# Batch 2's 1/rms by full matmuls with ones in place of column tiles and spreading DMAs, with a new order of the pieces

## The chip, the cores and the metric

The kernel runs on one core of one Trainium2 chip. The metric is the device time in microseconds (us) of one execution; the time before is the median of three runs.

## The reference

Per batch and head, an attention without softmax: kv = kᵀv (64 x 64), out = q·kv, divided by its root mean square over the head's 64 columns and scaled by g. The heads side by side are x; a channel mix follows.

```python
kv  = einsum('bhsd,bhse->bhde', k, v)
out = einsum('bhsd,bhde->bhse', q, kv)
x   = out / sqrt(mean(out * out, -1) + 1e-06) * g_norm      # heads side by side: (8, 576, 512)
x_prev = x one row later, zeros in front
xk = mu_k * x + (1 - mu_k) * x_prev;  xr = mu_r * x + (1 - mu_r) * x_prev
kk = maximum(xk @ w_k, 0.0);  v = kk * kk @ w_v;  r = sigmoid(xr @ w_r)
return r * v
```

Sizes: 8 batches, 8 heads, 576 rows, head width 64; 512 columns, 1024 in the hidden layer. Inputs and output are float32.

## The kernel before

The attention goes by batch (b = 0 to 7), each in two halves z of four heads, and for some steps in two parts i of 288 rows. The mix goes by group of 512 rows (g = 0 to 8). Group g needs the batches that its rows lie in: group 2 needs batches 1 and 2, group 3 batches 2 and 3, group 4 batches 3 and 4.

The code declares named pieces with their dependencies (`add`), and `plan.emit` issues them in the order of the words in `ORDER`. There is no other scheduler: each engine and each DMA queue works through its own pieces in that order, so a piece that waits holds up those behind it on the same engine. A suffix @A or @D puts a piece on ScalarE or VectorE. The words:

- `ldh.k`, `ldh.v`: batch 0's first half as float32 (SyncE's queue), and `cst.*`, the casts of it. `ld.*`: the other loads (GpSimd's queue, each waits there until its buffer is free); `ld.q0.zb` is the second half of a half's q.
- `kv`: kᵀv on TensorE (L274). `kc`: copy out of PSUM. `ks`: matmuls with a permutation (L280). `kd`: copy of the result. `tq`: q transposed on VectorE (L367). `u`: q·kv, transposed (L291).
- `uc`: u times g from PSUM into uT (L134 on ScalarE, L136 on VectorE). `sq`: squares (L389, ScalarE).
- `ss`: sums of squares by head, on TensorE. `rs`: 1/rms by one ScalarE instruction of 128 x 576 (L297). `mul`: x = uT * rs (L415; batch 0 from PSUM, L411). `d`: difference of neighbouring rows (L309). `mk`, `mr`: d times mu - 1. `xk`, `xr`: the blended inputs (L322; batch 0 L329).
- `k{g}.{fc}`: xk @ w_k (L517; group 0 L492, in parts). `relu` (L475, ScalarE), `ksq` (square, VectorE). `r{g}.{ci}`: xr @ w_r (L544). `sig` (L554, ScalarE). `v{g}.{ci}.{part}`: times w_v (L564). `out`: product (L577, L591). `st`: store (L466, SyncE).
- `z:512` and `zz`: matmuls of zeros that add nothing, while the first loads come (L460). `table`: first load of ScalarE's function table.

PSUM gives four buffers ("ps") that all pieces on TensorE share.

The sums of squares are done in one of two ways, by `CB`:

- Batches below CB: a full 128 x 128 matrix `ones` (1/64 within each head) sums the squares and puts the sum on all 64 partitions of its head. Batch 1 has four pieces `ss1.0` to `ss1.3`, each two matmuls of 288 columns (L418), and four passes `rs1.0` to `rs1.3`. The result lies as `mul` needs it.
- Batches from CB on: eight matmuls with the 128 x 32 matrix `heads` write four column tiles side by side (L398), so one piece `ss2` holds all heads and one pass `rs2` does all into `rsc`. Then `sp2.0` and `sp2.1` spread it over the partitions: four DMAs each on SyncE's queue (L440), 72 KB each. `mul2.z` waits for `sp2.z`.

CB is 2 before.

Of the kernel before, what the change touches and what calls it, by code (L numbers as in the profile page):

```python
# [56 lines left out]
def kernel(  # L57
# [283 lines left out]
    def attention(b):  # L341
# [64 lines left out]
        for z in range(NZ):  # L406
# [27 lines left out]
            ps_ = []  # L434
            if b >= CB:
                def spread(_, z=z, rs=rs):
                    for y in range(2):
                        for e in range(2):
                            r = 32 * (2 * z + y)
                            nc.sync.dma_start(out=get(rs)[64 * e:64 * e + 64, y, :],  # L440
                                              in_=rsc.t[r + e:r + 32:2, :].unsqueeze(1).to_broadcast([16, 4, S]))
# [191 lines left out]
```

## Time and profile before

| | us |
|---|---|
| median of 3 runs | 199.29 (199.22 to 199.31) |
| the profiled execution | 199.39 |
| its span | 197.5 |
| TensorE busy | 188.0 (95%) |
| VectorE busy | 134.0 (68%) |
| ScalarE busy | 127.0 (64%) |

The span is what the trace covers; 1.89 us of the execution lie around it. Times in the trace count from the span's start. PE is TensorE, DVE VectorE, ACT ScalarE, POOL GpSimd, SP SyncE; SPq is SyncE's DMA queue. Where a matmul record is missing from the trace, the timeline shows a gap of 0.16 us.

### The profile page before, as it was taken

The page shows a single profiled execution, that of the slowest core. Times are in us where ns is not written, and L with a number is a line of the kernel's source. Part 1 is how long each engine was busy: PE and PEld are TensorE (multiplying, and loading weights), DVE is VectorE, ACT ScalarE, POOL GpSimd, SP SyncE. Part 2 cuts the span into 40 slices and gives each one's busy share as a digit, 9 for nine tenths or more (in the row PEclk, how much of TensorE's full clock was granted, in tenths as well). Part 3 has the DMA queues.
Part 4 walks back from the last instruction along what each step waited for, and adds up shares of the span by engine and source line. Part 5 has one row for each costly group of instructions (what it writes and reads, how often), then busy time and mean ns, then how long its engine had stood idle before and what let it go on. Part 6 is the DMA issues. An engine that isn't in the chain of part 4 may idle for free.

```text
span 197.5 us, 4233 instructions
## 1 busy us (share of the span) xinstructions
PE 188.0 (95%) x1736; PEld 93.2 (47%) x1760; DVE 134.0 (68%) x227; ACT 127.0 (64%) x166; POOL 24.6 (12%) x44
## 2 busy tenths in 40 slices
PE   7987999999998999999999999999999999999992
PEld 2445864443534544344556554444444444444451
DVE  3389979888749699964997949876398440431272
ACT  3365599569989579889895876795518463342300
POOL 7842433041303000000000000000000000000000
PEclk9999999999999999999999999999999999999999
DMA  6999999999999999999632404413506003002226
GB/s 219 214 206 216 198 198 208 212 204 214 212 238 263 225 233 280 229 214 262 251 110 60 113 5 113 131 37 81 150 0 240 25 0 110 0 0 106 94 90 244
DMA packets 21192, 30.63 MB, mean 155 GB/s; under 512 B 1964, under 2 KB 14516, under 8 KB 21172
## 3 DMA queue, kind: packets, MB, share of 16 engines
...
q8 instruction: 14, 0.23, 0.5%
...
q14 instruction: 6, 0.05, 0.1%
...
## 4 chain that ended last, share of the span: by engine, by line
PE 73%; DMA 14%; DVE 6%; ACT 2%; issue 2%; SPq 1%; POOL 0%; DVEq 0%; ACTq 0%
PE ps L517 25%; PE ps L564 25%; PE ps L544 12%; DMA q<-in_q_dram 11%; PE ps L460 4%; DMA rs<-rsc 3%; PE ps L492 2%; PE ps L291 2%; PE ps L274 2%; DVE xT L411 1%; DVE qT L367 1%; ACT relu L475 1%; DVE xk L329 1%; DVE d L309 1%; PE ps L398 1%
## 5 line engine op out<-in xcount | busy, mean ns | idle before, releaser
L564 PE MATMUL ps<-w_v,sqk 128*128 128x512 bf16 (+1 forms) x286 | 66.0, 373 | 1.0 <-issue 0.6
L517 PE MATMUL ps<-xk,w_k 128*128 128x512 bf16 (+1 forms) x280 | 59.1, 355 | 1.4 <-DVE xk L322 0.7
L475 ACT ACTIVATE relu<-ps 128x1024 bf16<-128x1024 f32 x36 | 36.7, 1025 | 24.4 <-PE ps L517 18.5
L564 PEld LDWEIGHTS <-sqk 128*128 128x128 bf16 x296 | 28.3, 98 | 32.6 <-issue 1.8
L532 DVE TENSOR_TENSOR sqk<-relu 128x1024 bf16<-128x1024 bf16 x32 | 21.6, 686 | 29.6 <-ACT relu L475 22.4
L517 PEld LDWEIGHTS <-w_k 128*128 128x128 bf16 x288 | 27.2, 98 | 27.9 <-issue 1.8
L544 PE MATMUL ps<-w_r,xr 128*128 128x512 bf16 x140 | 33.8, 379 | 0.2
L554 ACT ACTIVATE sig<-ps 128x1024 bf16<-128x1024 f32 x18 | 18.5, 1025 | 15.9 <-DVE out L577 7.8
L577 DVE TENSOR_TENSOR out<-ps,sig 128x1024 f32<-128x1024 f32 x16 | 19.5, 1219 | 11.2 <-issue 5.7
L389 ACT ACTIVATE sq<-ps 128x576 bf16<-128x576 f32 x32 | 20.2, 652 | 4.1 <-PE ps L291 2.2
L544 PEld LDWEIGHTS <-xr 128*128 128x128 bf16 x144 | 13.7, 98 | 16.0 <-issue 0.7
L367 DVE STREAM_TRANSPOSE qT<-q 128x576 f32<-128x576 f32 (+1 forms) x20 | 14.7, 761 | 3.7 <-DMA q<-in_q_dram 3.5
...
L134 ACT ACTIVATE md<-d,cols 128x576 bf16<-128x576 bf16 x20 | 14.2, 769 | 1.7 <-DVE d L309 1.5
L309 DVE TENSOR_TENSOR d<-xT 128x1152 bf16<-128x1152 bf16 (+1 forms) x18 | 12.4, 691 | 0.4
L134 ACT ACTIVATE uT<-ps,cols 128x576 bf16<-128x576 f32 x16 | 11.7, 744 | 1.2 <-PE ps L291 1.2
L415 DVE TENSOR_TENSOR xT<-uT,rs 128x1152 bf16<-128x1152 bf16 x14 | 10.4, 744 | 2.1 <-DMA rs<-rsc 1.1
L136 DVE TENSOR_SCALAR md<-d,cols 128x576 bf16<-128x576 bf16 x36 | 11.3, 363 | 0.2
L136 DVE TENSOR_SCALAR uT<-ps,cols 128x576 bf16<-128x576 f32 x12 | 9.6, 814 | 2.7 <-ACT sq L389 2.5
L322 DVE TENSOR_TENSOR xk<-md,xT 128x1152 bf16<-128x1152 bf16 x14 | 10.5, 756 | 1.2 <-ACT md L134 0.9
L322 DVE TENSOR_TENSOR xr<-md,xT 128x1152 bf16<-128x1152 bf16 x14 | 10.5, 748 | 0.5 <-ACT md L134 0.4
L460 PE MATMUL ps<-zero 128*128 128x512 bf16 x28 | 9.3, 477 | 1.5 <-DVE ident L167 1.2
...
## 6 DMA issues: line engine op xcount, KB each, us to landing
...
k<-in_k_dram POOLq DMA_DIRECT2D x3, 288.0 KB, 12.9
```

The costliest lines, as they stand in the source:

```text
L134: nc.scalar.mul(out=dst, in_=src, mul=col)
L136: nc.vector.tensor_scalar(out=dst, in0=src, scalar1=col, scalar2=None, op0=ALU.mult)
L322: nc.vector.tensor_tensor(out=dst[:, 2 * z:2 * z + 2, r0:r0 + w], in0=md.t[:, :, cs], in1=xT[:, :, cur], op=ALU.add)
L389: sq_ = add("sq" + name, "A", lambda _, ps=ps, sq=sq, cs=cs, w=w: nc.scalar.activation(out=get(sq)[:, :, cs], in_=ps.t[:, :, 0:w], func=AF ...
L460: nc.tensor.matmul(get(k_ps[(0, 0)])[:, 0, 0:n], zero[:, 0:128], zero[:, 0:n], start=not started, stop=not started)
L475: nc.scalar.activation(out=get(rt), in_=ps.t, func=AF.Relu)
L517: nc.tensor.matmul(get(ps)[:, fc % 2, a0:a1], w_k_sb[:, cc, 128 * fc:128 * fc + 128], xk[:, cc, x0:x0 + a1 - a0], start=(cc == 0), stop=(c ...
L532: nc.vector.tensor_mul(out=get(sqk)[:, 2 * f2:2 * f2 + 2, :], in0=rt.t, in1=rt.t)
L544: nc.tensor.matmul(get(ps)[:, ci % 2, :], xr[:, cc, n0:n0 + 128], w_r_sb[:, cc, :], start=(cc == 0), stop=(cc == NHP - 1))
L554: nc.scalar.activation(out=get(sg), in_=ps.t, func=AF.Sigmoid)
L564: nc.tensor.matmul(get(ps)[:, bank, cs], sqk.t[:, fc, 128 * ci:128 * ci + 128], w_v_sb[:, fc, cs], start=(fc == 0), stop=(fc == NFC - 1))
L577: dv = add(f"out{g}.{c2}", "D", lambda _, ps=ps, sg=sg, ot=ot: nc.vector.tensor_mul(out=get(ot), in0=ps.t, in1=sg.t), deps=ms + [sg_done], ...
```

## The change

`CB` becomes 3, so batch 2 takes the first way: `ss2`, `rs2`, `sp2.0`, `sp2.1` are gone, and `ss2.0` to `ss2.3` and `rs2.0` to `rs2.3` come in. Batches 3 to 7 stay as they are. `ORDER` is written anew from end to end: most pieces change places, about twenty copies and scalings change between ScalarE and VectorE, and the number of zero matmuls stays 30. The core of the diff, with the stretches of `ORDER` that matter here:

```diff
-    CB = 2
+    CB = 3
```

The start of `ORDER`:

```diff
-ldh.k ldh.v ld.q0.0 ld.q0.0b ld.q0.1b seta setp ident perm ld.k0.1 ld.q0.1 ld.v0.1 ld.wk0 ld.v1.1 ld.wk1 ld.k1.1 ld.q1.1 ld.k1.0 ld.v1.0 ld.wr ld.q1.0 ld.wv0 ld.wv1 ld.k2.01 ld.v2.01 ld.q2.01 table small zz setb cst.k0@D cst.v0@D cst.k1@A cst.v1@A
...
+ldh.k ldh.v ld.q0.0 ld.v0.1 ld.q0.0b seta zz setp ident ld.q0.1 ld.k0.1 perm ld.q0.1b ld.wk0 ld.wk1 ld.v1.1 ld.k1.1 ld.q1.1 ld.k1.0 ld.v1.0 ld.wr ld.q1.0 ld.wv0 ld.wv1 ld.v2.01 ld.k2.01 ld.q2.01 small table cst.k1@A cst.k0@A tq0.0.0 setb cst.v0@A tq0.0.1 tq0.1.0 cst.v1@A
```

Batch 2's sums and on to group 2:

```diff
-ss2 rs2 uc2.10@A sp2.1 k1.5.1 relu1.2 r1.2 kv3.01 ld.v6.01 ld.k7.01 ld.q6.01 kc3.01@A r1.0 r1.3 sig1.1 ks3.01 kd3.01@D ksq1.2 r1.1 sig1.0 v1.1.0 u3.01.1 sq3.11 uc3.11@D sq3.01 v1.0.0 sp2.0 uc3.01@A v1.1.1 u3.01.0 sq3.10 sq3.00 v1.3.0 uc3.00@A v1.0.1 mul2.1 st0.3 uc3.10@A v1.2.0 kv5.01 ld.k6.01 ld.v7.01 ss3 d2.1 mk2.1@D xk2.1 v1.3.1 mul2.0 d2.0 st0.2 rs3 sp3.0 v1.2.1 mk2.0@D xk2.0 kc5.01@A mr2.0@A sp3.1 mr2.1@A ks5.01 kd5.01@D k2.4
...
+r1.2 tq3.01.0 uc2.10@D ksq1.3 ss2.2 rs2.2 st0.0 ksq1.2 ksq1.1 r1.3 ss2.3 ss2.1 rs2.3 rs2.1 r1.0 ss2.0 r1.1 kv3.01 rs2.0 v1.1.0 mul2.1 d2.1 mk2.1@D kc3.01@D ks3.01 tq3.01.1 ld.q6.01 ld.v7.01 xk2.1 mul2.0 sig1.1 sig1.0 kd3.01@A v1.0.0 v1.1.1 u3.01.1 mr2.1@A sq3.01 v1.0.1 uc3.01@A uc3.11@D v1.3.0 out1.0 sq3.11 v1.3.1 kv5.01 u3.01.0 sq3.00 uc3.00@A kc5.01@A d2.0 mk2.0@D xk2.0 v1.2.0 v1.2.1 st0.1 k2.0 k2.1 out1.1 ks5.01 relu2.0 kd5.01@D tq4.01.1 uc3.10@D k2.2 k2.3 relu2.1 k2.4 sq3.10 k2.6
```

Batch 3's sums and on to group 3, new order only:

```diff
+kv4.01 ksq2.1 ss3 ksq2.0 rs3 sp3.1 k2.5 sp3.0 st1.1 tq4.01.0 ld.q7.01 ld.v6.01 ld.k7.01 ld.k6.01 relu2.2 k2.7 kc4.01@D ks4.01 kd4.01@A tq5.01.1 v2.1.0 ksq2.2 relu2.3 st1.0 u4.01.1 ksq2.3 sq4.11 xr2.1 v2.0.0 v2.3.0 sq4.01 uc4.01@D v2.1.1 mr2.0@D xr2.0 uc4.11@A u4.01.0 sq4.10 sq4.00 v2.3.1 st0.2 v2.0.1 mul3.1 st0.3 v2.2.0 v2.2.1 d3.1 uc4.00@A ss4 mk3.1@D uc4.10@A xk3.1 r2.0 r2.1 rs4 sp4.1 r2.2 r2.3 mul3.0 d3.0 mk3.0@D xk3.0 sig2.0 out2.0 k3.0
```

In the old order `ss3` and `rs3` stand ahead of group 2, as the stretch before this one shows, and group 3 begins with `k3.2` after `ss4` and `rs4`.

More of the change, by code (lines that the diff above doesn't have):

```diff
@@ L15 @@
 ORDER = """
-ldh.k ldh.v ld.q0.0 ld.q0.0b ld.q0.1b seta setp ident perm ld.k0.1 ld.q0.1 ld.v0.1 ld.wk0 ld.v1.1 ld.wk1 ld.k1.1 ld.q1.1 ld.k1.0 ld.v1.0 ld.wr ld.q1.0 ld.wv0 ld.wv1 ld.k2.01 ld.v2.01 ld.q2.01 table small zz setb cst.k0@D cst.v0@D cst.k1@A cst.v1@A z:512 z:512 z:512 z:512 z:512 z:512 z:512 z:512 z:512 z:512 z:512 z:512 z:512 z:512 z:512 z:512 kv0.0 kc0.0@A z:512 z:512 ks0.0 kd0.0@A tq0.0.0 tq0.0.1 z:512 z:512 u0.0.1 u0.0.0 tr9 sq0.00 cols tq0.1.1 z:512 z:512 ss0.00 tq0.1.0 rs0.00 mul0.00 d0.00 xk0.00 z:512 z:512 z:512 z:512 kv0.1 ld.k3.01 ld.v3.01 ld.q3.01 sq0.01 ss0.01 kc0.1@A rs0.01 ks0.1 kd0.1@A z:512 z:512 z:512 u0.1.0 sq0.10 u0.1.1 sq0.11 k0.000 mul0.01 d0.01 xk0.01 xr0.01 ss0.10 rs0.10 mul0.10 d0.10 xk0.10 ss0.11 rs0.11 mul0.11 k0.010 k0.100 k0.001 relu0.00 k0.011 relu0.01 d0.11 xk0.11 xr0.11 kv1.1 kc1.1@D k0.101 ks1.1 kd1.1@A tq1.1.0 tq1.1.1 relu0.10 k0.110 u1.1.0 ksq0.00 u1.1.1 sq1.10 xr0.10 uc1.11@A kv1.0 ld.k5.01 ld.v5.01 kc1.0@A uc1.10@D sq1.11 xr0.00 tq1.0.0 k0.111 relu0.11 ss1.3 rs1.3 tq1.0.1 ss1.2 ks1.0 ksq0.11 r0.2 r0.3 rs1.2 r0.0 mul1.1 kd1.0@A u1.0.1 u1.0.0 sig0.1 sq1.00 r0.1 ksq0.10 sq1.01 uc1.01@A sig0.0 v0.1.0 d1.1 ksq0.01 v0.0.0 v0.0.1 mk1.1@D xk1.1 ss1.1 uc1.00@D v0.1.1 out0.0 rs1.1 ss1.0 rs1.0 v0.3.0 v0.3.1 v0.2.0 v0.2.1 mul1.0 d1.0 mk1.0@D kv2.01 ld.k4.01 ld.v4.01 ld.q4.01 kc2.01@A xk1.0 k1.0.0 k1.6.0 mr1.0@A out0.1 k1.7.0 k1.6.1 ks2.01 kd2.01@A tq2.01.0 tq2.01.1 ld.q5.01 k1.7.1 xr1.0 relu1.3 k1.1.0 k1.0.1 u2.01.1 sq2.11 uc2.01@D k1.2.0 k1.1.1 uc2.11@D sq2.01 relu1.0 k1.3.0 mr1.1@D xr1.1 k1.2.1 u2.01.0 sq2.00 k1.3.1 uc2.00@D ksq1.3 k1.4.0 k1.5.0 sq2.10 tq3.01.0 relu1.1 ksq1.1 tq3.01.1 k1.4.1 ksq1.0 ss2 rs2 uc2.10@A sp2.1 k1.5.1 relu1.2 r1.2 kv3.01 ld.v6.01 ld.k7.01 ld.q6.01 kc3.01@A r1.0 r1.3 sig1.1 ks3.01 kd3.01@D ksq1.2 r1.1 sig1.0 v1.1.0 u3.01.1 sq3.11 uc3.11@D sq3.01 v1.0.0 sp2.0 uc3.01@A v1.1.1 u3.01.0 sq3.10 sq3.00 v1.3.0 uc3.00@A v1.0.1 mul2.1 st0.3 uc3.10@A v1.2.0 kv5.01 ld.k6.01 ld.v7.01 ss3 d2.1 mk2.1@D xk2.1 v1.3.1 mul2.0 d2.0 st0.2 rs3 sp3.0 v1.2.1 mk2.0@D xk2.0 kc5.01@A mr2.0@A sp3.1 mr2.1@A ks5.01 kd5.01@D k2.4 k2.5 out1.1 st1.2 xr2.0 k2.2 relu2.2 k2.0 k2.1 ksq2.2 xr2.1 relu2.0 kv4.01 st0.0 k2.3 kc4.01@D ksq2.0 k2.6 ks4.01 k2.7 relu2.1 out1.0 ksq2.1 tq4.01.1 kd4.01@A st1.3 r2.2 tq4.01.0 ld.q7.01 mul3.0 relu2.3 st0.1 ksq2.3 r2.0 r2.1 sig2.0 u4.01.0 uc4.10@A d3.0 mr3.0@D r2.3 v2.2.0 sq4.10 v2.2.1 sig2.1 mk3.0@D uc4.00@A tq5.01.0 tq5.01.1 sq4.00 v2.1.0 v2.3.0 u4.01.1 uc4.01@A sq4.01 v2.3.1 v2.0.0 mul3.1 uc4.11@A d3.1 v2.1.1 xk3.0 mk3.1@D xk3.1 sq4.11 out2.1 ss4 rs4 k3.2 k3.3 sp4.1 sp4.0 mr3.1@D xr3.1 relu3.1 v2.0.1 u5.01.1 uc5.11@A uc5.01@A out2.0 st2.0 xr3.0 st2.1 sq5.01 k3.6 k3.7 st1.1 sq5.11 k3.0 relu3.3 st1.0 ksq3.1 u5.01.0 uc5.10@A sq5.10 tq6.01.1 k3.1 relu3.0 st2.3 r3.0 ksq3.3 r3.1 sig3.0 k3.4 ksq3.0 k3.5 v3.0.0 kv7.01 relu3.2 uc5.00@D kv6.01 sq5.00 ss5 kc6.01@A mul4.1 d4.1 mk4.1@D rs5 v3.1.0 kc7.01@A ksq3.2 v3.1.1 ks6.01 kd6.01@A xk4.1 mul4.0 d4.0 v3.0.1 out3.0 st3.0 tq7.01.0 mk4.0@D xk4.0 mr4.1@A v3.3.0 ks7.01 kd7.01@A mr4.0@A r3.2 xr4.0 tq6.01.0 v3.2.0 r3.3 sig3.1 k4.0 k4.1 relu4.0 u6.01.1 xr4.1 sq6.01 v3.2.1 k4.6 st2.2 v3.3.1 ksq4.0 uc6.01@D k4.2 uc6.11@D k4.7 sq6.11 out3.1 relu4.3 u6.01.0 tq7.01.1 sp5.1 mul5.1 sq6.10 d5.1 mk5.1@D k4.3 uc6.10@A r4.0 r4.1 st3.3 relu4.1 mr5.1@D ksq4.1 r4.2 r4.3 sq6.00 ksq4.3 uc6.00@D sig4.0 sig4.1 k4.4 k4.5 v4.1.0 relu4.2 u7.01.0 ksq4.2 sp5.0 xk5.1 xr5.1 ss6 rs6 v4.0.0 sp6.1 v4.0.1 v4.1.1 mul5.0 d5.0 mk5.0@A out4.0 sq7.10 xk5.0 uc7.10@D v4.3.0 mr5.0@A xr5.0 sq7.00 st3.2 mul6.1 sp6.0 uc7.00@A v4.3.1 v4.2.0 v4.2.1 out4.1 k5.2 st4.2 k5.3 k5.6 k5.7 relu5.1 ksq5.1 relu5.3 d6.1 u7.01.1 sq7.01 uc7.01@D uc7.11@A k5.4 k5.5 relu5.2 sq7.11 mk6.1@A k5.0 mul6.0 r5.2 ksq5.2 k5.1 ksq5.3 relu5.0 r5.0 ss7 r5.1 st4.0 xk6.1 rs7 sp7.0 ksq5.0 v5.3.0 v5.2.0 v5.3.1 d6.0 r5.3 sig5.1 mk6.0@D v5.2.1 xk6.0 st3.1 mr6.0@D k6.2 k6.3 relu6.1 k6.6 k6.7 st4.3 relu6.3 v5.1.0 v5.1.1 ksq6.1 sig5.0 v5.0.0 v5.0.1 k6.4 k6.5 out5.1 mul7.0 k6.0 k6.1 relu6.0 xr6.0 mr6.1@D xr6.1 r6.2 sp7.1 mul7.1 d7.1 r6.3 r6.0 d7.0 r6.1 out5.0 st5.1 mr7.0@A ksq6.0 mr7.1@A mk7.1@D mk7.0@D v6.1.0 ksq6.3 xk7.0 xk7.1 sig6.1 v6.0.0 relu6.2 st5.3 xr7.0 k7.0 k7.1 relu7.0 ksq6.2 v6.1.1 k8.4 k8.5 relu8.2 ksq8.2 k7.4 k7.5 relu7.2 xr7.1 v6.0.1 k7.2 k7.3 k7.6 sig6.0 st4.1 st5.2 st5.0 out6.0 st6.0 st6.1 v6.3.0 v6.2.0 relu7.1 r8.2 r8.3 sig8.1 v6.3.1 k8.0 k8.1 v6.2.1 ksq7.2 ksq7.0 ksq7.1 relu8.0 ksq8.0 k7.7 relu7.3 k8.2 k8.3 r8.0 ksq7.3 r8.1 sig8.0 relu8.1 r7.0 r7.1 ksq8.1 v7.1.0 out6.1 st6.2 st6.3 v7.3.0 v7.0.0 v7.3.1 v7.2.0 v7.0.1 r7.2 sig7.0 r7.3 v7.1.1 out7.0 st7.0 st7.1 k8.6 k8.7 sig7.1 v8.2.00 relu8.3 v8.1.00 v8.0.00 ksq8.3 v7.2.1 out7.1 st7.2 st7.3 v8.0.10 out8.00 st8.00 v8.2.10 out8.20 st8.20 v8.1.10 out8.10 st8.10 v8.3.01 v8.3.11 out8.31 st8.31 v8.3.00 v8.3.10 out8.30 st8.30
@@ new lines @@
+ldh.k ldh.v ld.q0.0 ld.v0.1 ld.q0.0b seta zz setp ident ld.q0.1 ld.k0.1 perm ld.q0.1b ld.wk0 ld.wk1 ld.v1.1 ld.k1.1 ld.q1.1 ld.k1.0 ld.v1.0 ld.wr ld.q1.0 ld.wv0 ld.wv1 ld.v2.01 ld.k2.01 ld.q2.01 small table cst.k1@A cst.k0@A tq0.0.0 setb cst.v0@A tq0.0.1 tq0.1.0 cst.v1@A z:512 z:512 z:512 z:512 z:512 z:512 z:512 z:512 z:512 z:512 z:512 z:512 z:512 z:512 kv0.0 kc0.0@A z:512 z:512 ks0.0 tr9 kd0.0@A u0.0.0 sq0.00 z:512 z:512 z:512 ss0.00 cols kv0.1 rs0.00 kc0.1@A tq0.1.1 ld.q3.01 ld.v3.01 ld.k3.01 mul0.00 d0.00 xr0.00 xk0.00 z:512 u0.0.1 ks0.1 sq0.01 z:512 z:512 ss0.01 kd0.1@A u0.1.0 rs0.01 mul0.01 sq0.10 z:512 z:512 z:512 z:512 ss0.10 rs0.10 mul0.10 z:512 z:512 z:512 u0.1.1 d0.10 xk0.10 sq0.11 k0.010 d0.01 ss0.11 rs0.11 k0.000 k0.001 k0.011 mul0.11 d0.11 xk0.01 xk0.11 relu0.00 tq1.1.0 kv1.1 relu0.01 k0.100 k0.101 kc1.1@A tq1.1.1 xr0.10 xr0.11 ks1.1 k0.110 kd1.1@A u1.1.1 relu0.10 u1.1.0 kv1.0 ld.v5.01 ld.k5.01 k0.111 uc1.11@A ksq0.00 kc1.0@D ks1.0 sq1.10 sq1.11 uc1.10@D kd1.0@D ksq0.10 xr0.01 tq1.0.1 ss1.2 relu0.11 tq1.0.0 ksq0.11 ss1.3 rs1.3 r0.0 r0.1 rs1.2 sig0.0 r0.2 r0.3 mul1.1 u1.0.0 u1.0.1 sig0.1 uc1.01@D v0.1.0 ksq0.01 sq1.00 v0.2.0 sq1.01 ss1.0 uc1.00@D rs1.0 v0.3.0 ss1.1 d1.1 rs1.1 v0.0.0 mk1.1@D xk1.1 v0.0.1 mr1.1@A mul1.0 v0.3.1 d1.0 mk1.0@D xk1.0 v0.1.1 out0.0 mr1.0@A xr1.0 v0.2.1 out0.1 k1.0.0 k1.1.0 k1.0.1 k1.1.1 relu1.0 kv2.01 ld.v4.01 ld.q4.01 ld.k4.01 kc2.01@A k1.6.0 xr1.1 k1.2.0 tq2.01.0 ks2.01 kd2.01@A k1.7.0 k1.6.1 tq2.01.1 ld.q5.01 k1.7.1 k1.3.0 relu1.3 u2.01.1 sq2.11 ksq1.0 k1.2.1 uc2.01@D k1.4.0 sq2.01 k1.3.1 uc2.11@D k1.5.0 relu1.1 u2.01.0 sq2.10 uc2.00@D k1.4.1 k1.5.1 sq2.00 relu1.2 r1.2 tq3.01.0 uc2.10@D ksq1.3 ss2.2 rs2.2 st0.0 ksq1.2 ksq1.1 r1.3 ss2.3 ss2.1 rs2.3 rs2.1 r1.0 ss2.0 r1.1 kv3.01 rs2.0 v1.1.0 mul2.1 d2.1 mk2.1@D kc3.01@D ks3.01 tq3.01.1 ld.q6.01 ld.v7.01 xk2.1 mul2.0 sig1.1 sig1.0 kd3.01@A v1.0.0 v1.1.1 u3.01.1 mr2.1@A sq3.01 v1.0.1 uc3.01@A uc3.11@D v1.3.0 out1.0 sq3.11 v1.3.1 kv5.01 u3.01.0 sq3.00 uc3.00@A kc5.01@A d2.0 mk2.0@D xk2.0 v1.2.0 v1.2.1 st0.1 k2.0 k2.1 out1.1 ks5.01 relu2.0 kd5.01@D tq4.01.1 uc3.10@D k2.2 k2.3 relu2.1 k2.4 sq3.10 k2.6 kv4.01 ksq2.1 ss3 ksq2.0 rs3 sp3.1 k2.5 sp3.0 st1.1 tq4.01.0 ld.q7.01 ld.v6.01 ld.k7.01 ld.k6.01 relu2.2 k2.7 kc4.01@D ks4.01 kd4.01@A tq5.01.1 v2.1.0 ksq2.2 relu2.3 st1.0 u4.01.1 ksq2.3 sq4.11 xr2.1 v2.0.0 v2.3.0 sq4.01 uc4.01@D v2.1.1 mr2.0@D xr2.0 uc4.11@A u4.01.0 sq4.10 sq4.00 v2.3.1 st0.2 v2.0.1 mul3.1 st0.3 v2.2.0 v2.2.1 d3.1 uc4.00@A ss4 mk3.1@D uc4.10@A xk3.1 r2.0 r2.1 rs4 sp4.1 r2.2 r2.3 mul3.0 d3.0 mk3.0@D xk3.0 sig2.0 out2.0 k3.0 k3.1 tq5.01.0 k3.2 mr3.0@D sig2.1 out2.1 st2.3 relu3.0 xr3.0 k3.3 k3.4 mr3.1@D xr3.1 relu3.1 ksq3.1 sp4.0 ksq3.0 st1.2 k3.5 st1.3 tq7.01.1 relu3.2 ksq3.2 st2.2 u5.01.1 sq5.01 sq5.11 k3.6 uc5.01@A r3.0 k3.7 uc5.11@D relu3.3 r3.1 sig3.0 v3.1.0 ksq3.3 tq7.01.0 kv7.01 kc7.01@A u5.01.0 tq6.01.0 v3.0.0 v3.0.1 uc5.00@A sq5.10 mul4.1 st2.0 sq5.00 d4.1 mk4.1@D v3.1.1 uc5.10@A mr4.1@D ks7.01 kd7.01@A kv6.01 ss5 rs5 sp5.0 mul4.0 d4.0 mk4.0@D v3.2.0 v3.2.1 xr4.1 xk4.1 out3.0 r3.2 r3.3 sig3.1 kc6.01@A v3.3.0 v3.3.1 ks6.01 kd6.01@A xk4.0 k4.4 out3.1 mr4.0@D k4.5 relu4.2 k4.2 tq6.01.1 u6.01.1 sq6.01 uc6.11@D sq6.11 uc6.01@D sp5.1 mul5.1 ksq4.2 d5.1 k4.0 k4.1 relu4.0 u6.01.0 xr4.0 ksq4.0 k4.3 relu4.1 ksq4.1 uc6.00@A k4.6 k4.7 r4.2 r4.3 relu4.3 uc6.10@D ksq4.3 v4.3.0 mr5.1@D xr5.1 v4.3.1 sq6.00 sig4.1 sq6.10 u7.01.0 ss6 rs6 st2.1 sq7.10 sp6.1 v4.2.0 v4.2.1 mul5.0 uc7.00@D d5.0 sq7.00 mk5.0@D r4.0 mr5.0@A out4.1 st4.3 uc7.10@D st4.2 r4.1 v4.0.0 u7.01.1 sig4.0 st3.3 xk5.0 v4.1.0 v4.0.1 uc7.01@A uc7.11@A sq7.11 sq7.01 xr5.0 v4.1.1 mk5.1@D xk5.1 st3.0 k5.6 k5.7 relu5.3 mul6.1 d6.1 out4.0 ss7 sp6.0 rs7 k5.4 k5.5 mul6.0 d6.0 mr6.0@D mr6.1@D mk6.0@D xr6.1 st4.1 xk6.0 r5.0 mk6.1@D relu5.2 st3.2 r5.1 k5.2 sig5.0 k5.0 k5.3 relu5.1 k5.1 xk6.1 r5.2 ksq5.1 r5.3 relu5.0 k6.6 ksq5.2 ksq5.3 k6.7 sp7.1 k6.0 relu6.3 ksq5.0 k6.1 relu6.0 ksq6.0 v5.3.0 v5.3.1 v5.2.0 st4.0 k6.4 k6.5 sig5.1 v5.2.1 sp7.0 mul7.0 d7.0 mk7.0@D v5.1.0 v5.1.1 mul7.1 d7.1 mk7.1@D xk7.1 mr7.1@A xk7.0 xr6.0 relu6.2 ksq6.2 out5.1 st5.3 v5.0.0 st5.2 v5.0.1 out5.0 k8.2 k8.3 relu8.1 mr7.0@D k7.4 xr7.0 ksq6.3 k7.5 relu7.2 k7.2 k7.3 relu7.1 k7.6 ksq7.1 k6.2 k6.3 relu6.1 ksq6.1 r6.2 r6.3 sig6.1 k8.0 st3.1 k8.1 k7.0 k7.1 xr7.1 r7.0 r7.1 relu8.0 ksq7.2 k7.7 relu7.0 v6.3.0 v6.3.1 ksq7.0 relu7.3 v6.2.0 v6.2.1 r6.0 v7.2.0 out6.1 st6.2 st6.3 v7.3.0 ksq7.3 r6.1 v6.1.0 v6.0.0 v7.3.1 v6.0.1 sig6.0 v6.1.1 out6.0 st6.0 st6.1 st5.1 v7.2.1 k8.4 k8.5 relu8.2 ksq8.1 sig7.0 v7.0.0 v7.0.1 k8.6 k8.7 ksq8.2 relu8.3 v7.1.0 v7.1.1 out7.0 st7.0 st7.1 r7.2 r7.3 sig7.1 r8.2 r8.3 ksq8.0 v8.0.00 v8.1.00 out7.1 st7.2 st7.3 sig8.1 r8.0 ksq8.3 st5.0 r8.1 sig8.0 v8.2.00 v8.2.10 out8.20 v8.1.10 out8.10 st8.10 st8.20 v8.0.10 out8.00 st8.00 v8.3.00 v8.3.01 v8.3.11 out8.31 v8.3.10 st8.31 out8.30 st8.30
```

## The prediction

> **What bounds the kernel now.** I read the page first, for the busiest engine and the DMA row; then the chain of waits in order of time, for where that engine really stops; then TensorE's timeline for what one piece costs; last the DMA issues by stretch, because the change takes DMAs away.
>
> ```profile
> span 197.5 us, 4233 instructions
> ...
> PE 188.0 (95%) x1736; PEld 93.2 (47%) x1760; DVE 134.0 (68%) x227; ACT 127.0 (64%) x166; POOL 24.6 (12%) x44
> ...
> DMA  6999999999999999999632404413506003002226
> ```
>
> TensorE is busy for 95% of the span. A slice of the DMA row is 4.9 us, so the transfers are dense until about 99 us (twenty slices). From 18 us to 194 us TensorE's timeline shows one stop longer than a lost record (0.16 us): before 63.96. The chain says why:
>
> ```profile
> 54.29 6.27 DMA rs<-rsc
> ...
> 60.87 0.76 DVE xT L415
> 61.64 0.02 issue
> 61.66 0.77 DVE d L309
> 62.43 0.02 issue
> 62.46 0.66 DVE md L136 x2
> 63.12 0.02 issue
> 63.14 0.77 DVE xk L322
> 63.91 0.05 issue
> 63.96 4.49 PE ps L517 x20
> ```
>
> That is batch 2: the spread of 1/rms (sp2.0) lands at 60.56, then mul, d, mk and xk take 3.1 us to the first k2 matmul. TensorE had ended ks5.01 at 63.10 (it starts at 62.87 and such a piece takes 0.22), so it lost 0.86.
>
> So the time is TensorE's work, plus its stops, plus a fixed head and tail. I price the change on these.
>
> **TensorE's work.** Batch 2 gets four pairs of full matmuls for eight column tiles:
>
> ```profile
> 35.10 0.41 PE L418 MATMUL ps<-sq,ones 128*128 128x288 bf16 x2
> 35.34 1.03 PE L564 MATMUL ps<-w_v,sqk 128*128 128x512 bf16 x4
> ...
> 48.48 0.43 PE L398 MATMUL ps<-sq,heads 128*32 128x288 bf16 x8
> 48.85 0.60 PE L517 MATMUL ps<-xk,w_k 128*128 128x512 bf16 x2
> ```
>
> Start to next start: 0.24 for a pair, 0.37 for eight tiles. 4 x 0.24 - 0.37 = **+0.6**. Both orders hold 30 filler matmuls with zeros, and every other TensorE piece is the same, so this is all of it. The Trainium skill (TensorEngine Tiling (Array Packing), Theoretical Speedup) speaks against the edit more strongly: 32 columns give up to 4x, so undoing it would cost 4 x 0.37 = 1.48, or +1.1. The trace shows 2.6x; the measured pair decides.
>
> **The removed wait.** mul2.1 and mul2.0 now wait for passes on ScalarE. The 0.86 goes: **-0.9**. What is late next there: I follow the new order from r0.0 at 27.85 (below). TensorE's pieces by their rows add up to 13.2 as far as kv2.01 (41.1), 23.8 to the end of ss2.0 (51.65) and 33.8 to k2.0 (62.0 with 0.3 for changes of shape). rs2.0, 0.74 by L297 and behind rs2.1, ends at about 52.6. On VectorE xk2.0 follows u3.01.1 (to 56.8) by uc3.11 0.8, out1.0 1.2, d2.0 0.8, mk2.0 0.7 and its own 0.8: 61.1. That leaves 0.9 to spare. Bounds: -0.9 to 0.
>
> **ScalarE.** 4 x 0.74 for 1 x 0.74 is +2.2, before a table load (1.28), two sigmoids (2.1) and kd3.01 (0.37). From rs2.0's end at 52.6 that gives 56.4 for kd3.01. TensorE, from the end of ss2.0 at 51.65, has r1.1 0.87, kv3.01 0.70, v1.1.0 0.87, ks3.01 0.22, v1.0.0 and v1.1.1 1.73 and up to 0.3 for changes of shape (before, a v piece of 0.87 ahead of a u piece took from 53.82 to 54.78): 56.0 to 56.3 for u3.01.1, which needs kd3.01. The cover is just used up: **+0.2** (0 to 0.4; all further delay of ScalarE would show).
>
> **The first 40 us.** The fillers ahead of kv0.0 are two fewer, but all four casts (cst) are now on ScalarE, one after the other: the last ends at about 7.2 and kv0.0 starts as before (7.24). tq0.1.1, which needs a later load (ld.q0.1b), now stands before mul0.00 on VectorE: mul0.00 goes from 12.1 to about 12.4, and xk0.11, the last of batch 0, from 21.9 to about 22.2. TensorE does not feel it: k1.1 lands at 20.9 (8.00 + 12.9), w_r at 27.8 (11.88 + 15.9). Before, TensorE stood 0.83 and 0.48 at 16.5 to 18.3 and began its first r piece at 28.34; the new order has done the same work (22.1 us by rows, both) when w_r lands, so r0.0 starts at about 27.85: **-0.5**. Bounds: -0.7, and +0.5 if the load of q0.1b comes later than 11.6.
>
> **The spread that stays.** Batch 3 keeps its column tiles and eight spreading DMAs, and its place moves. Before, rs3 ended at 62.0 and k3 began at 85.9: 24 us. Now ss3 stands after kv4.01, and k3.0 soon after. Between lie, on TensorE: k2.5 and k2.7 1.73, ks4.01 0.23, v2 pieces 8 x 0.865 = 6.92, two u4 0.76, three changes of shape 0.3, ss4 0.37, four r2 3.46: 13.8. rs3 ends 0.86 after ss3 (48.85 to 49.71 for batch 2). Cover: 12.9.
>
> What has to fit: eight issues on SyncE, the landing of the last, 0.3 until mul starts, 3.1 from mul3.0 to k3.0.
>
> ```profile
> 49.73 5.97 SPq L440 DMA_DIRECT2D rs<-rsc  x8
> ...
> 62.07 5.81 SPq L440 DMA_DIRECT2D rs<-rsc  x8
> ...
> 84.42 5.69 SPq L440 DMA_DIRECT2D rs<-rsc  x8
> ```
>
> The eighth starts 5.2 after rs ends. While loads fill the DMAs it lands late: issues of 62 to 68 us have a median of 7.8 (8.3 at the end), of 84 to 90 us 6.8 (6.3 at the end); batch 2's last group was there 10.9 after rs. So the second group lands 10.9 (batch 2), 11.6 (batch 4) or 13.6 (batch 3) after rs ends. In the new order this lies at 70 to 84 us, still inside the loads: after q2 (42.3) they land 2.8 apart, k4 at about 66, and q5, q6, v7, q7, v6, k7, k6 follow, to about 88. I take the middle: 11.6 + 0.3 + 3.1 - 12.9 = **+2.1** (1.4 to 4.1). Queued behind the waiting mul3.1 and mul3.0 on VectorE are out2.0, tq5.01.0 and out2.1, whose PSUM the next pieces get after k3.0; TensorE waits at k3.0 itself.
>
> Other moves: on SyncE the stores st0.0 and st0.1 no longer stand behind sp2 and go out at about 40; as DMAs they take what two groups of sp2 took, so k4 is no later than kv4.01 needs it (68). sp4.0 comes to stand behind st2.3, which needs out2.1: it lands at about 96, and k4.4 is due past 103. POOL's loads change places only among neighbours, and each lands before its kv or tq by 1 us or more. tq4.01.1 on VectorE waits for q4, at about 64, when VectorE gets to it. The tail runs the same pieces in the same distance from the end. These I cost at nothing; the cover named is what they have.
>
> **Sum.** 0.6 - 0.9 + 0.2 - 0.5 + 2.1 = +1.5. The profiled execution took 199.39 (span 197.5 and 1.9 around it), 0.1 over the median 199.29: 200.9 on its own scale, **200.8** as a median.
>
> **Rivals.**
> - Batch 3's spread lands in time (no stop at k3.0): +0.6 - 0.9 + 0.2 - 0.5 = -0.6, **198.7**. For it: issues of 100 to 105 us land in 2.1, so 5.2 + 2.1 + 0.3 + 3.1 = 10.7 fits into 12.9. It decides if the loads are through, or thin, by 75 us. Against: twelve loads followed q3 (50.8) until 94 before, and only 0.6 MB of spreads go away. The Trainium skill (DMA: Bandwidth & Descriptors, Anatomy of one DMA) gives about 2.0 us plus bytes over 436 GB/s, 2.2 for 72 KB, fitted on transfers that GpSimd issues; by it this rival holds. The trace agrees after 100 us and not before 95.
> - A second stop in front as well: q0.1b lands late, or ScalarE's four passes take a wait more, and 1 us is lost where I count a gain of 0.5 or a loss of 0.2. With k3.0's stop: **202.2**. It decides when kv1.1 starts after 22.5 or u3.01.1 more than 1 us late.
> - The change does not take the wait away: VectorE's own queue, uc3.11 and out1.0 ahead of d2.0, holds xk2.0 back and k2.0 waits 0.9 as before. ss3 moves along with it, so k3.0's stop stays: 0.6 + 0.2 - 0.5 + 2.1 = +2.4, **201.7**. It decides if out1.0 starts after 59.
>
> **How the numbers follow.** A measurement of this kernel can tell about 0.2%, 0.4 us, from no change. Chances: forecast 0.56, no stop at k3.0 0.25, second stop 0.11, wait not removed 0.08. Faster takes 0.22 of the second; same, between 198.9 and 199.7, takes the other 0.03 and 0.03 of the forecast's low end; slower has the rest: 0.22, 0.06, 0.72. The likeliest case alone spans 199.7 to 203.0 (1.4 to 4.1 at k3.0 with the front's bounds). Over the cases I give 198.6 to 203.0.
>
> **What would show it.** L398 falls from 48 to 40 matmuls, L418 rises from 16 to 24, SyncE's spreads from 48 to 40. Right: xk2.0 ends a microsecond before k2.0; the first 128x512 matmul of L517 in group 3 shows 1.4 to 4 idle, released by VectorE's xk (L322); VectorE's mul before it (L415) idle, released by DMA rs<-rsc. Wrong: no idle there and spreads of 70 to 76 us landing in under 5; or a stop of over 0.5 us elsewhere after 20 us.

## The result and the profile after

Four runs of the changed kernel have a median of 201.59 us (201.53 to 201.85), four of the kernel before, on the same chip, 199.3 (199.22 to 199.9). The ratio is 1.0111, 95% interval 1.0089 to 1.0132: slower by 1.1%, where 200.8 was predicted. The span grew by 2.3 us, from 197.5 to 199.8.

The page first, the lines that answer to those of before:

```profile
span 199.8 us, 4218 instructions
...
PE 188.1 (94%) x1738; PEld 94.0 (47%) x1760; DVE 139.6 (70%) x240; ACT 122.0 (61%) x156; POOL 24.7 (12%) x44
...
DMA  6999999999999999998315005733004000230515
```

TensorE is as busy as before, in a longer span: it stands more. The transfers are dense for nineteen slices, a slice less than before. VectorE has 5.6 us more and ScalarE 5.0 less, mostly because copies and scalings changed engine.

The chain of waits shows where TensorE stands, a stretch that has the same shape as the chain before 63.96 had, twenty microseconds later:

```profile
73.80 0.55 SPq L440
...
75.03 0.59 SPq L440
...
75.67 6.61 DMA rs<-rsc
...
82.64 0.76 DVE xT L415
...
83.43 0.77 DVE d L309
...
84.22 0.66 DVE md L136 x2
...
84.91 0.77 DVE xk L322
...
85.72 2.33 PE ps L517 x10
```

SyncE issues batch 3's eight spreads one after the other, the last at 75.67; it lands at 82.27, and mul3.0, d, mk and xk take it to k3.0 at 85.72. TensorE's timeline, the first matmul of each row at the left, the idle time ahead of it and its releaser in brackets:

```profile
62.99 1.89 PE L517 MATMUL ps<-xk,w_k 128*128 128x512 bf16 x8
...
69.19 0.43 PE L398 MATMUL ps<-sq,heads 128*32 128x288 bf16 x8
...
79.85 1.90 PE L544 MATMUL ps<-w_r,xr 128*128 128x512 bf16 x8
83.17 1.89 PE L544 MATMUL ps<-w_r,xr 128*128 128x512 bf16 x8 [1.42 <-ACT rsc L297]
85.72 4.49 PE L517 MATMUL ps<-xk,w_k 128*128 128x512 bf16 x19 [0.67 <-DVE xk L322]
```

The stop before k2.0 is gone (62.99, nothing in brackets). ss3 runs at 69.19, and 14 us later TensorE stands twice: before r2.2 and before k3.0. r2.0 to r2.3 should take 4 x 0.865 = 3.46, and 85.72 - 79.85 is 5.87: the two stops cost 2.41 from start to start. The brackets add up to 2.09, since idle time counts from a modelled end.

k3.0 waits for its xk. That r2.2 waits for rs4 (L297 into rsc) is a second face of the same wait. On ScalarE's timeline:

```profile
82.38 0.74 ACT L297 ACTIVATE rsc<-ps,eps 128x576 bf16<-128x576 f32 x1 [3.83 <-DMA rs<-rsc]
```

There is one buffer for rsc. rs4 may write it only when sp3.0's last DMA has read it, so it waits until 82.27. Until then ss4's sums stay in their PSUM buffer, and r2.2 needs a buffer.

### The profile page after: what moved, and what is told of

The parts are those of the page before. It is cut to its first block, busy times and chain, and to the rows that moved or that the text cites. A ratio compares the mean times of both kernels' runs of the same rounds, so it can differ in the third digit from the quotient of the medians.

```text
span 199.8 us, 4218 instructions
## 1 busy us (share of the span) xinstructions
PE 188.1 (94%) x1738; PEld 94.0 (47%) x1760; DVE 139.6 (70%) x240; ACT 122.0 (61%) x156; POOL 24.7 (12%) x44
## 3 DMA queue, kind: packets, MB, share of 16 engines
q1 hardware_dynamic: 8948, 13.44, 20.9%
## 4 chain that ended last, share of the span: by engine, by line
PE 79%; DMA 13%; DVE 2%; issue 2%; SPq 1%; ACT 1%; POOL 0%; DVEq 0%; ACTq 0%; POOLq 0%
PE ps L517 28%; PE ps L564 28%; PE ps L544 14%; DMA k<-in_k_dram 6%; DMA rs<-rsc 3%; DMA q<-in_q_dram 3%; PE ps L274 3%; PE ps L291 3%; PE ps L492 2%; PE ps L418 1%; PE ps L280 1%; SPq L440 1%; PE ps L398 1%; ACT relu L475 0%; DVE out L591 0%
## 5 line engine op out<-in xcount | busy, mean ns | idle before, releaser
L517 PE MATMUL ps<-xk,w_k 128*128 128x512 bf16 (+1 forms) x280 | 58.4, 355 | 1.4 <-DVE xk L322 0.7
L136 DVE TENSOR_SCALAR uT<-ps,cols 128x576 bf16<-128x576 f32 x16 | 12.9, 809 | 3.0 <-PE ps L291 3.0
L136 DVE TENSOR_SCALAR md<-d,cols 128x576 bf16<-128x576 bf16 x46 | 14.6, 365 | 0.4
L460 PE MATMUL ps<-zero 128*128 128x512 bf16 x28 | 8.6, 448 | 1.4 <-DVE ident L167 1.2
L297 ACT ACTIVATE rs<-ps,eps 128x576 bf16<-128x576 f32 x12 | 8.6, 740 | 1.9 <-PE ps L418 1.7
L134 ACT ACTIVATE md<-d,cols 128x576 bf16<-128x576 bf16 x10 | 7.2, 775 | 3.8 <-DVE d L309 3.8
```

The lines of the kernel that those rows point to most:

```text
L136: nc.vector.tensor_scalar(out=dst, in0=src, scalar1=col, scalar2=None, op0=ALU.mult)
L517: nc.tensor.matmul(get(ps)[:, fc % 2, a0:a1], w_k_sb[:, cc, 128 * fc:128 * fc + 128], xk[:, cc, x0:x0 + a1 - a0], start=(cc == 0), stop=(c ...
```

## The experiments

Each kernel ran on one chip together with the kernel before; ratios are to that. Not all ran on the same chip: the kernel before took 199.5 to 199.8 us beside them, so ratios compare better than times. The theory was: the last landing of batch 3's spread, late because the loads share the DMAs, sets k3.0, and moving ss3 in the new order brought it about. The rivals were the single rsc buffer, the method by full matmuls itself, and the new tail and front.

**A second buffer for rsc.**

```diff
-"rsc": (1, (128, S), BF16)
+"rsc": (2, (128, S), BF16)
```

> The changed kernel with two buffers for rsc instead of one; nothing else. Theory: both stops after 81 us (1.42 at r2.2, 0.67 at k3.0) come from one landing, the last DMA of batch 3's spread; rs4 waits for it only because rsc has one buffer. With two, r2.2 starts at once and k3.0 waits the whole 2.1: time unchanged, 201.4 to 201.8, idle before the first k3 matmul 1.9 to 2.3. Rival: the single rsc buffer is itself the loss, and 1.4 is gained: 200.2, with 0.7 left at k3.0.

Ratio 1.0163 (1.0104 to 1.0222), runs 201.37 to 203.56 us. No stop is left at r2.2; TensorE's timeline has all of it at k3.0:

```profile
79.58 3.63 PE L544 MATMUL ps<-w_r,xr 128*128 128x512 bf16 x16
85.74 4.49 PE L517 MATMUL ps<-xk,w_k 128*128 128x512 bf16 x19 [2.53 <-DVE xk L322]
```

r2.0 began 0.27 earlier than in the changed kernel, r2.2 did not wait, and k3.0 begins at 85.74 against 85.72. The buffer only chooses where TensorE waits; the landing sets when it goes on. From k3.0 to TensorE's end both kernels take 109.95. The profile is of a run of 201.59. The two longer runs, 203.27 and 203.56 us, have a mean granted TensorE clock of 0.992, the other two 1.000; where in those runs the clock fell is not recorded. All four runs lie above the rival's 200.2.

**Fewer loads.** Batches 6 and 7 use the tiles of 4 and 5, so the loads of two batches are left out.

```diff
-    kvq = {(n, b): Buf(n) for n in "kvq" for b in range(B)}
+    kvq = {(n, b): Buf(n) for n in "kvq" for b in range(B - 2)}
+    for n in "kvq":
+        for b in (6, 7):
+            kvq[(n, b)] = kvq[(n, b - 2)]
```

and the words `ld.q6.01` to `ld.k7.01` go.

> The changed kernel without the six loads of batches 6 and 7 (q, k, v): those two batches work on the tiles of batches 4 and 5 again, all instructions on the engines stay. So the DMAs have no loads after q5, at about 70 us, when batch 3's spread begins. Theory: the spread lands late because loads fill the DMAs; here each of its DMAs lands in 2 to 3.5 us instead of 6.6, xk3.0 is ready before k3.0 is due and both stops go: 199.3 to 199.7. Rival: the eight issues one after the other and the chain on VectorE are the price: landing still 5 or more, stop of 1.5 or more, 201.0 to 201.7.

Ratio 0.9952 (0.9936 to 0.9969), 198.5 us. The DMA issues from 70 to 76.5 us, median us to landing last; first the changed kernel, then this one:

```profile
rs<-rsc SPq DMA_DIRECT2D x8, 72.0 KB, 6.6
```

```profile
rs<-rsc SPq DMA_DIRECT2D x8, 72.0 KB, 2.1
```

Without the loads the same spreads land in 2.1, and both stops are gone. So the loads make the landing late, and the late landing makes the stops. The time fell by 3.1 where 2.1 was expected. The traces place the rest: r0.0 began at 28.00 instead of 28.36, because k1.1 landed 0.36 earlier (20.91 against 21.27), long before the left-out loads were due; and the end of the program, from TensorE's last matmul on, took 3.6 instead of 4.1 (see the tail below).

**Batch 3's sums earlier, all else in the new order.**

```diff
-uc3.10@D k2.2 k2.3 relu2.1 k2.4 sq3.10 k2.6 kv4.01 ksq2.1 ss3 ksq2.0 rs3 sp3.1 k2.5 sp3.0
+k2.2 k2.3 relu2.1 k2.4 k2.6 kv4.01 ksq2.1 ksq2.0 k2.5
```

with `ss3 rs3 sp3.1 sp3.0` put ahead of `ks5.01`, and `sq3.10` and `uc3.10@D` up behind `sq3.00` and `xk2.0`.

> The changed kernel with ss3, rs3, sp3.1 and sp3.0 moved ahead of ks5.01, some 4.5 us earlier (sq3.10 and uc3.10 moved forward to allow it). Theory: with the spread 4.5 us earlier, its last DMA lands at about 78 and both stops (2.1) are gone, nothing else lost: 199.3 to 199.8. Rival: ScalarE is needed for relu2.0 just there; rs3 with its table load ahead of it delays PSUM, and a new stop of 1 or more comes at k2.2 or k2.4: 200.5 or more.

Ratio 0.9986 (0.9974 to 0.9998), 199.26 us over ten runs: no stop is left, and the kernel is level with the one before. Its SyncE queue and, after that, its TensorE timeline:

```profile
66.00 5.16 SPq L440 DMA_DIRECT2D rs<-rsc  x8
```

```profile
64.75 0.43 PE L398 MATMUL ps<-sq,heads 128*32 128x288 bf16 x8
...
79.90 3.63 PE L544 MATMUL ps<-w_r,xr 128*128 128x512 bf16 x16
83.36 5.34 PE L517 MATMUL ps<-xk,w_k 128*128 128x512 bf16 x23
```

The spreads land no faster (6.5 median in 62 to 76 us), but they leave 4.6 us earlier. r2.0 begins where it did, 0.05 apart, and k3.0 2.36 earlier: the stops' whole price.

**The new order with batch 2 by column tiles.**

```diff
-    CB = 3
+    CB = 2
...
-ss2.2 rs2.2 st0.0 ksq1.2 ksq1.1 r1.3 ss2.3 ss2.1 rs2.3 rs2.1 r1.0 ss2.0 r1.1 kv3.01 rs2.0 v1.1.0
+ss2 rs2 sp2.1 sp2.0 st0.0 ksq1.2 ksq1.1 r1.3 r1.0 r1.1 kv3.01 v1.1.0
```

> The new order with the method undone: batch 2 by column tiles, one pass and eight spreading DMAs again, at the place where the change begins its four pairs. Theory: the method takes a wait away: here rs2 ends at about 50.8, the spread's last DMA lands 10.9 later at about 61.7, xk2.0 is ready at about 65 and k2.0, due at 62.5, waits 2 to 3; TensorE saves 0.6, the stops at batch 3 stay, since ss3 moves along: 203.0 to 204.0. Rival: the full matmuls and passes themselves cost the time and the old way is hidden in this order too: 200.6 to 201.2.

Ratio 1.0506 (1.0483 to 1.053), 209.59 us: I had missed what stands behind mul2.1. VectorE's timeline, then TensorE's:

```profile
59.55 0.76 DVE L415 TENSOR_TENSOR xT<-uT,rs 128x1152 bf16<-128x1152 bf16 x1 [7.58 <-DMA rs<-rsc]
```

```profile
62.17 0.59 PE L280 MATMUL ps<-kvn,perm 128*128 128x128 bf16 x4 [7.56 <-DVE kvn L130]
62.55 3.62 PE L564 MATMUL ps<-w_v,sqk 128*128 128x512 bf16 x8
```

kc3.01, the copy that ks3.01 needs, is on VectorE behind a mul2.1 that waits 7.58 for its spread. The stop costs more than its length: in its last two microseconds and the four after it, from 60 to 66 us, the granted TensorE clock was 0.50, and eight 128x512 matmuls took 3.62 where the changed kernel's took 1.89. The kernel answers what that queue costs, not what the method is worth, so I undid that too:

```diff
-rs2.0 v1.1.0 mul2.1 d2.1 mk2.1@D kc3.01@D ks3.01 tq3.01.1 ld.q6.01 ld.v7.01 xk2.1 mul2.0 sig1.1
+kc3.01@A v1.1.0 ks3.01 tq3.01.1 ld.q6.01 ld.v7.01 sig1.1
...
-out1.0 sq3.11 v1.3.1
+out1.0 sq3.11 mul2.1 d2.1 mk2.1@D xk2.1 v1.3.1
```

(on top of the edit above; `mr2.1@A` and `mul2.0` follow `kc5.01@A`).

> The new order with the method undone for batch 2 (column tiles, one pass, eight spreading DMAs), and this time the pieces that would stand behind mul2.1 on VectorE and are needed at once are taken out of its way: kc3.01 goes to ScalarE, tq3.01.1 and uc3.11, out1.0 go ahead of mul2.1, mr2.1 goes behind kc5.01. Theory: rs2 ends at about 51, the last DMA lands 10.9 later, k2.0 (due at 62.4) starts at about 65: 201.6 - 0.6 + 2.7 = 203.7, from 203.0 to 204.3. Rival: the old way is hidden here too: 200.6 to 201.2.

Ratio 1.0286 (1.0269 to 1.0302), 205.5 us, a little over the range expected. On TensorE:

```profile
66.86 1.89 PE L517 MATMUL ps<-xk,w_k 128*128 128x512 bf16 x8 [3.33 <-DVE xk L322]
```

k2.0 begins 3.87 later than in the changed kernel (66.86 against 62.99). The stop of 3.33 is what the spread costs there; a stop of 1.09 at u3.01.1, ahead of it, waits for kd3.01 on ScalarE, which my moving kc3.01 there helped to delay, and it does not add to the time, as k2.0 waits for xk2.0 either way. The stops at batch 3 are 0.78 and 0.75. By the ratios (1.0286 and 1.0111) the full matmuls are worth 3.5 us in this order. That is the value in an order made for them.

**The full matmuls in the old order.** Three tries, each with CB = 3 and `sp2` left out:

```diff
-ss2 rs2 uc2.10@A sp2.1 k1.5.1 relu1.2 r1.2 kv3.01
+ss2.2 rs2.2 uc2.10@A ss2.3 rs2.3 k1.5.1 relu1.2 r1.2 ss2.0 ss2.1 kv3.01
```

with `rs2.0 rs2.1` behind `kc3.01@A`;

> The method alone: the kernel before with CB 3, its old order kept but for the four pairs and four passes, which stand near the old ss2 and rs2 (two passes behind kc3.01). Theory: TensorE +0.6, the 0.86 ahead of k2 gone: 199.0, from 198.9 to 199.4 (the upper end if the 2.2 on ScalarE delay squares of batch 3 and with them PSUM). Rival: the four passes cost more on ScalarE than the wait was worth: 200.0 or more, with a stop of TensorE between 51 and 60.

the second with the pairs spaced as in the new order (r1.3, r1.0, r1.1 and ksq1.2 go up between them, and v1.1.0 goes ahead of ks3.01);

```diff
-ss2 rs2 uc2.10@A sp2.1 k1.5.1 relu1.2 r1.2 kv3.01
+uc2.10@A k1.5.1 relu1.2 r1.2 ss2.2 rs2.2 ksq1.2 r1.3 ss2.3 rs2.3 ss2.1 rs2.1 r1.0 ss2.0 rs2.0 r1.1 kv3.01
```

> The method alone once more: the kernel before with CB 3, but with the new order's local sequence around the four pairs (r1.2, ss2.2, r1.3, ss2.3, ss2.1, r1.0, ss2.0, r1.1, kv3.01), so that each pass on ScalarE has an r piece of 0.87 beside it and no PSUM buffer waits; everything else as before. Theory: the three stops of the first try (1.8) came from PSUM held by the pairs, not from the method; now TensorE +0.6 and the 0.86 ahead of k2 gone: 199.0 on the scale where before is 199.3, ratio 0.997 to 1.000. Rival: ScalarE's 2.2 more comes out somewhere, with kd3, sq3 or relu: ratio 1.004 or more.

and the third as the second, with batch 3's loads in the new sequence:

```diff
-ld.k3.01 ld.v3.01 ld.q3.01
+ld.q3.01 ld.v3.01 ld.k3.01
```

> The second try of the method alone, with one more edit: batch 3's loads go out as q, v, k instead of k, v, q, as the new order has them. In the second try group 0's stores, no longer behind sp2 on SyncE, went out at 42.4 instead of 55.8 and q3 landed at 52.6 instead of 50.9; VectorE stood for tq3.01.0, and TensorE 0.54 and 0.59 behind ksq1 and kd3.01. Theory: with q3 first, tq3.01.0 does not wait, kv3.01 (due at 53.9) still finds k3, and both stops go: TensorE's end 1.1 earlier than in the second try, ratio 0.998 to 1.003. Rival: ScalarE's four passes are behind the two stops: they stay, ratio 1.005 or more.

Ratios 1.0088 (1.0074 to 1.0101), 1.0068 (1.0051 to 1.0086) and 1.0088 (1.0068 to 1.0108): slower, all three, though the stop before k2 is gone in each. In the first, PSUM buffers wait for relu and rs on ScalarE (stops 0.18, 0.51 and 1.13). In the first two, q3 lands at 52.56 and 52.58 instead of 50.85: st0.0 and st0.1, no longer behind sp2 in SyncE's queue, go out from 41.6 and 42.4 on, beside the loads, instead of 55.8. That the stores delay q3 is likely, but no run separates them. With q3 loaded first, the third still stops for 1.31. On TensorE, and then on ScalarE:

```profile
56.32 0.32 PE L291 MATMUL ps<-qT,kv 32*64 32x288 bf16 x4 [0.58 <-DVE kv L130]
57.37 0.44 PE L291 MATMUL ps<-qT,kv 32*64 32x288 bf16 x12 [0.73 <-ACT sig L554]
```

```profile
54.61 0.37 ACT L128 CAST kvn<-ps 128x256 bf16<-128x256 f32 x1 [0.86 <-PE ps L274]
```

u3.01.1 waits for the copy kd3.01, and then for a PSUM buffer that sig1 frees. The four passes are not what is late: they end at 53.75, and ScalarE then stands 0.86 until kv3.01 is done; kc3.01, a table load and sig1 follow. What changed is the order: r1.0, r1.1, r1.3 and v1.1.0, which came between kv3.01 and u3.01.1 in the old order, stand ahead of kv3.01 or of ks3.01 now, so nothing is left between ks3.01 (55.35) and u3.01.1 to cover the copy and sig1. So the third try, and the second with its stop of 0.59 at the same place, price their own order as much as the method; in the first, the stops wait for ScalarE itself. What the method would be worth in the best order near the old one stays open.

**Batch 3 by full matmuls too.**

```diff
-    CB = 3
+    CB = 4
```

with four pairs in the places of ss3 and the pieces behind it.

> The changed kernel with CB 4: batch 3 by full matmuls and four passes as well, its spread gone, the pairs laid between k2.5, k2.7, ks4.01 and v2.1.0. Theory of one stop: the spread's 2.1 goes and 0.6 of TensorE comes in: 200.1. Rival, from the first try in the old order: the pairs hold PSUM buffers until ScalarE has made its passes, and stops of 0.5 to 1.8 come in at ks4.01 to v2.1.0: 200.6 to 201.9.

Ratio 1.01 (1.0082 to 1.0117). No stop is left at r2.2 or k3.0, but kv4.01 waited for k4:

```profile
69.95 0.78 PE L274 MATMUL ps<-v,k 64*64 64x64 bf16 x72 [1.93 <-DMA k<-in_k_dram]
```

k4 landed at 69.9 there, at 67.0 in the changed kernel. With sp3 gone from SyncE's queue, four stores of 256 KB go out at 59.7 to 61.2 instead of from 77.1 on, beside the loads; the later landing goes with them, as q3's did in the old order. So the time does not say what the method is worth for batch 3.

**The tail.** The old order of the last pieces:

```diff
-v8.3.00 v8.3.01 v8.3.11 out8.31 v8.3.10 st8.31 out8.30 st8.30
+v8.3.01 v8.3.11 out8.31 st8.31 v8.3.00 v8.3.10 out8.30 st8.30
```

and `st8.20` directly behind `out8.20`.

> The changed kernel with the last pieces in the old sequence: st8.20 ahead of st8.10, v8.3.01, v8.3.11, out8.31 and its store ahead of v8.3.00. From TensorE's end to the span's end the changed kernel takes 4.13 against 3.68. Theory: that 0.45 comes from the sequence (out8.31 right ahead of out8.30, three stores together): 201.1 to 201.25. Rival: it lies in the end of the program, after the last store, and the sequence is worth nothing: 201.5 to 201.7.

Ratio 1.0092 (1.0077 to 1.0107); the changed kernel's interval overlaps, so the time does not decide. VectorE's last rows, first the changed kernel, then this one:

```profile
195.27 0.86 DVE L591 TENSOR_TENSOR out<-ps,sig 128x256 f32<-128x256 f32 x2 [0.62 <-PE ps L564]
```

```profile
195.47 0.42 DVE L591 TENSOR_TENSOR out<-ps,sig 128x256 f32<-128x256 f32 x1 [0.45 <-PE ps L564]
```

In the changed kernel the last two products run back to back; here they are 0.87 apart (194.60 and 195.47). But the last product ends 0.46 after TensorE's last matmul in both (196.13 - 195.67 and 195.89 - 195.43), and 0.45 after it in the kernel before. So the 0.45 that the changed kernel takes longer lies behind the last product. There, at L628, which stands behind the whole kernel, SyncE's queue waits for TensorE's queue (PEq). In total, how often and the longest wait, in us; first the kernel before, then the changed kernel, the third try in the old order, and the run with fewer loads (whose lines are shifted by six):

```profile
SPq L628 <- PEq L628: 0.7, 2, 0.5
SPq L628 <- PEq L628: 1.2, 2, 1.0
SPq L628 <- PEq L628: 1.1, 2, 1.0
SPq L634 <- PEq L634: 0.6, 2, 0.5
```

The longest of these waits is 0.5 in some profiles and 1.0 in others, and the order of the last pieces does not choose: the third try has the old order and 1.0, the run with fewer loads the changed one and 0.5. From TensorE's end to the span's end it is 3.6 to 3.7 in the four profiles with 0.5, and 3.9 to 4.2 in the ten with 1.0, this run (4.0) among them. So the rival holds for most of the 0.45: it lies in the end of the program. What sets that wait is open. What the old sequence is worth, 0.1 to 0.2 in the traces, is not clear of the noise.

**Both: batch 3's sums earlier, and the old tail.** Edits as above.

> ss3, rs3 and the spread of batch 3 moved forward as before, and the old tail as well. Theory: both gains add up: 199.26 - 0.45, so 198.7 to 198.9. Rival (tail worth nothing): 199.1 to 199.4.

Ratio 0.9969 (0.9958 to 0.9981), 199.05 us against 199.66: faster than both kernels, by 0.3% than the one before. Its interval overlaps that of the run with batch 3's sums alone (0.9974 to 0.9998), so the tail's part in this is not shown. The same two edits, with two of the first casts on VectorE:

```diff
-cst.k1@A cst.k0@A tq0.0.0 setb cst.v0@A tq0.0.1 tq0.1.0 cst.v1@A
+cst.k1@A cst.k0@D cst.v0@D tq0.0.0 setb cst.v1@A tq0.0.1 tq0.1.0
```

> The changed order with ss3 moved forward and the old tail, and the casts of batch 0 shared again between VectorE and ScalarE, as before, so that kv0.0 need not wait for four casts in a row on ScalarE (1.38 idle ahead of it). Theory: the front is bound by the landing of k1.1 at 21.3, which kv1.1 waits for, so 0.3 to 0.6 won at kv0.0 is lost there: same time as without this edit, ratio 0.995 to 0.999. Rival: the front is bound by its chain from kv0.0 on, and 0.4 or more is won: ratio 0.993 to 0.995.

Ratio 0.999 (0.9968 to 1.0011), runs from 198.75 to 202.44. kv0.0 starts at 6.48 instead of 7.41 in the run above, and u0.0.0 then waits 1.24 for q's transpose, so the gain is gone when kv0.1 starts (11.36 in both). The profile is of one of three longer runs (201.04): its granted TensorE clock was 0.50 from 11 to 17 us, so the front's end can't be read from it. The mean clock of the three is 0.981 to 0.983, and of the other nine, which took 198.75 to 199.48, 0.996 or more.

## Why the prediction was right, and where its steps were not

Direction and mechanism held: the stop at k2 goes, and a late spread of batch 3 costs more than that. The size was 0.8 us short (2.3 instead of 1.5), and it is partly luck that it was no more: the front, the spread and the end of the program came out 1.25 dearer than forecast, ScalarE and small places on TensorE 0.5 cheaper. By its own signs the place was only half right: k3.0 shows 0.67 idle where 1.4 to 4 was named, and the 1.42 at r2.2 is one of the stops "elsewhere" that were named as a sign of being wrong.

- **TensorE's work, +0.6.** L398 has 40 matmuls and L418 24. In the new order a pair takes 0.24 (49.80 to 50.04 on TensorE's timeline). Right.
- **The removed wait, -0.9.** k2.0 follows without idle time. xk2.0 ended at 61.98, 1.0 ahead of it (0.9 predicted). Right.
- **The spread that stays, +2.1.** 2.4 from start to start. The last landing came 11.7 after rs3 ended, where the middle of three rows gave 11.6. VectorE stood 3.16 at mul3.1, for the DMA. What the step missed is the ring behind it: rsc's single buffer and ss4's PSUM, by which more than half showed at r2.2. It changed the place and not the sum, as the second buffer showed: with it all of the wait, 2.53, is at k3.0. One reading was wrong, but the sum does not use it: before, k3 began at 82.83 (k3.2, right behind ss4 at 82.47), not at 85.9, so the old cover was 20.8 us and not 24. That the rival without a stop fell, and why, is in the run with fewer loads. By the Trainium skill (DMA: Bandwidth & Descriptors, Anatomy of one DMA) a 72 KB transfer takes an estimated 2.2 us (the page's fit is of transfers that GpSimd issues, these are SyncE's); the run without the loads agrees (2.1), the kernel itself does not (6.6), so the page's figure holds here only while no loads share the DMAs.
- **The first 40 us, -0.5.** This step failed: r0.0 began at 28.36, against 28.34 before. The walk had TensorE done with its work when w_r lands (27.8), and it was not. kv1.1 began at 21.31, as k1.1 landed at 21.27 (20.9 predicted), and from there to r0.0 TensorE worked without a stop for 7.05. In the run with fewer loads k1.1 did land at 20.91, the same pieces took 7.05 again, and r0.0 began at 28.00. So 0.36 of the 0.5 hang on that landing; the other 0.15 is work that the sum by rows had too short.
- **ScalarE, +0.2.** No stop at u3.01.1 in the new order, though the cover was as thin as was said: kd3.01 ended at 56.96 and u3.01.1 began at 57.08. The term was not wrong in kind: in the first try in the old order a stop of 1.13 waits for a pass.
- **The tail, 0.** 0.45 came from TensorE's end to the span's end. The pieces do run in the same distance: the last product ends 0.45 and 0.46 after TensorE. What was not priced is the end of the program, where one wait took 1.0 instead of 0.5; it differs between profiles with the same tail, and its cause is open.
- **Stores and loads at nothing.** Right in the new order: k4 landed at 67.0, 1.5 ahead of kv4.01. The other runs show what early stores can go with: q3 later by 1.7 in the old order, k4 later by 2.9 with batch 3 by full matmuls.

The sum as it came out: 0.6 - 0.86 + 2.41 + 0.45 = 2.6, and 2.3 measured; 0.3 that TensorE gained in small places was not followed. Two figures of the prediction do not follow from its own terms: the second stop's 202.2 would be 202.3 in front or 201.6 at ScalarE, and the likeliest case's upper end, with the front's bound, is 203.8 and not 203.0. Neither touches the forecast.

The change thus does what it says: it takes the wait at k2. Its loss is the new place of ss3, which no part of the method needs, and the runs undo it.
